# Talking-heads attention and a squared-ReLU FFN: 128-column weights for two matmuls, and another way out for the last output tile

## Chip, cores and metric

The kernel runs on one core of a Trainium2 chip. The metric is the device time of one execution in microseconds. A core has five engines that work side by side, each through its own list of instructions: TensorE (PE, matmuls; its weight loads are shown apart as PEld), VectorE (DVE), ScalarE (ACT), GpSimd (POOL) and SyncE (SP). Transfers run on DMA engines and are issued by GpSimd, SyncE or ScalarE.

## The reference

Eight batches, 12 heads, 448 positions, head size 64. Scores are mixed across the heads before the softmax (w_pre) and again after it (w_post); the result of the attention, 3584 tokens by 768, goes through a feed-forward layer with 2048 inner features.

```python
scores = scale * np.matmul(q, k.transpose(0, 1, 3, 2))
scores = np.einsum('bhij,hg->bgij', scores, w_pre)
scores = scores - np.max(scores, axis=-1, keepdims=True)
attn = np.exp(scores)
attn = attn / (np.sum(attn, axis=-1, keepdims=True) + 1e-09)
attn = np.einsum('bhij,hg->bgij', attn, w_post)
x = np.matmul(attn, v)          # then (b, s, h*d): 3584 x 768
h = np.maximum(x @ w_in, 0.0)   # 768 x 2048
out = h * h @ w_out             # 2048 x 768
```

## The kernel before

A planner in Python puts all work in order before the program is built: each matmul group is a unit, and the planner decides by estimated times which unit TensorE takes next. The built program has a fixed order on every engine.

A batch is handled in chunks of 10 query rows by 12 heads, which is 120 rows (NR). The steps are:

- T: q and k are transposed by TensorE (L610), two heads on top of each other in 128 partitions (`qkt`).
- QK: for a row tile of 12 chunks and a pair of heads, two matmuls, one for the head in partitions 0 to 63 and one for the head in 64 to 127 (L734). The weights are the columns of q, the stream is all 448 columns of k. Both results are copied to `stage`.
- A move by DMA, issued by SyncE (L781), brings a chunk of `stage` into the order "10 rows by 12 heads" on 120 partitions (`dring`).
- Pre-mix: one matmul for each chunk with a block matrix of w_pre as weights (L809), then the exponential with row sums on ScalarE (L827). The first 10 chunks of batch 0 take a direct way (L683).
- Post-mix: four matmuls for each chunk (L873) with w_post scaled by the inverse row sum (L843), then attention times v (L935).
- FFN: the first layer (L994), ReLU, square, second layer (L1076), eviction to `osb`, store.

QK, with the weights i0:i1 of a row tile (the row tiles are 120, 120, 120 and 88 rows; in batch 0 110, 120 and 118, behind the direct chunks):

```python
i0, i1 = ca * CH, min(cb * CH, S)
nr = i1 - i0
...
for par in range(2):
    r0 = par * 64
    r_ = eng.matmul(
        ps[0:nr, banks[par], 0:S],
        qkt[r0:r0 + 64, pb, p, 0, i0:i1],       # weights: 64 rows, nr columns
        qkt[r0:r0 + 64, pb, p, 1, :],           # stream: 448 columns
        start=True, stop=True,
    )
```

Pre-mix:

```python
wk1 = sb("wk1", [NR, CH, H], DT.bfloat16)       # 120 x 120
...
return eng.matmul(ps[0:NR, bank, 0:S], wk1[:, :, :], dring[:, slot, :],
                  start=True, stop=True)
```

The end of an output tile (128 tokens by 768, in two halves of 384 columns): after the second half the whole tile is stored by GpSimd, in as many pieces as the rows of the output need. The last tile, number 3 of the last batch, holds 64 rows of each of two batches and leaves in two pieces:

```python
t_oe = add("oev%d_%d_%d" % (b, tile, hh), FLEX, fn_oe, ...)   # eviction of a half
if hh == 1:
    if b % 2 and tile == 3:
        spans = ((0, b, 384, 448), (64, b - 1, 384, 448))
    ... # cut: pieces of the rows
    def fn_od(eng, en, s=s, pieces=tuple(pieces)):
        for p0, m, row in pieces:
            dst = bass.AP(out.tensor, row * F, [[RJ * F, m], [OP, 4], [1, OP]])
            eng.dma_start(dst, osb[p0:p0 + m, s, :, 0:OP]).then_inc(
                sem_out[s].handle, 16)
    t_od = plan.add("odma%d_%d" % (b, tile), POOL, fn_od,
                    [oev_of[(b, tile, 0)], t_oe], ...)
```

At the very end SyncE waits for the semaphores of all stores.

Of the kernel before, what the change touches and what calls it, by code (L numbers as in the profile page):

```python
# [8 lines left out]
DT = mybir.dt  # L9

PE = "pe"
ACT = "act"
DVE = "dve"
POOL = "pool"
SP = "sp"
FLEX = "flex"
ENGINE_NAMES = (PE, ACT, DVE, POOL, SP)
SEM_LAT = 60.0
MODE_SWITCH = 100.0
ACT_BIAS = 50.0  # L20
MARGIN = 500
MARGIN_DMA = 4000
# [59 lines left out]
class _Plan:  # L82
# [19 lines left out]
    def add(self, name, engine, fn, deps=(), cost=None, prio=0.0, sem=None, seminc=0,  # L102
# [11 lines left out]
        if engine == PE:  # L114
            assert t.nwait == 0
            start = max(self.free[PE], t.avail)
            if t.mode != self.mode:
                start += MODE_SWITCH
                self.mode = t.mode
# [55 lines left out]
    def take(self, n):  # L175
        _, got = self.find(n, self.free[PE])
        self.taken.update(got)
        return got, [t for i in got for t in self.bank_users[i]]
# [11 lines left out]
    def _pick(self):  # L190
# [4 lines left out]
        for s in self.streams:  # L195
# [15 lines left out]
            if u.mode != self.mode:  # L211
                est += MODE_SWITCH
            if est < INF:
# [54 lines left out]
def bass_talking_heads_attention__then__ffn_squared_relu_kernel(  # L268
# [10 lines left out]
    B, H, S, D = q.shape  # L279
    F, FF = moe_w_in.shape  # L280
    assert H == 12 and D == 64 and F == H * D and S == 448 and B % 2 == 0
    CH = 10
    NR = CH * H
# [10 lines left out]
    RJ = 4  # L294
    JB = S // RJ
    NFT = F // 128
    NFFT = FF // 128
    FH = F // 2
# [5 lines left out]
    with ExitStack() as es:  # L304
        def sb(name, shape, dtype):
            return es.enter_context(nc.sbuf_tensor(name, list(shape), dtype))

        def pp(name, shape, dtype):
            return es.enter_context(nc.psum_tensor(name, list(shape), dtype))
# [5 lines left out]
        OP = F // 4  # L315
# [12 lines left out]
        wrep = sb("wrep", [NR, 2, H], DT.float32)  # L328
        wq = sb("wq", [128, NP, H], DT.float32)
        wall = sb("wall", [128, NP, 2, H], DT.float32)  # L330
        wk1 = sb("wk1", [NR, CH, H], DT.bfloat16)
        wk2b = sb("wk2b", [NR, H, CH], DT.bfloat16)
        wk2s = sb("wk2s", [NR, NWS, NR], DT.bfloat16)
        rowsum = sb("rowsum", [NR, NPS, 1], DT.float32)
# [6 lines left out]
        qkt = sb("qkt", [128, 2, NP, 2, S], DT.bfloat16)  # L341
        stage = sb("stage", [IT, 2, H, S], DT.bfloat16)
        dring = sb("dring", [NR, NDS, S], DT.bfloat16)
# [6 lines left out]
        osb = sb("osb", [128, NOS, 4, OP + 8], DT.float32)  # L350

        NB = 8
        ps = pp("ps", [128, NB, 512], DT.float32)
        ps_bf = ps.bitcast(DT.bfloat16)

        def Sm(name):
            return _Sem(nc.alloc_semaphore(name), name)
# [6 lines left out]
        sem_wq = Sm("dwq")  # L364
        sem_w = [[Sm("dw%d_%d" % (i, j)) for j in range(NWP)] for i in range(2)]
        sem_dsl = [Sm("dsl%d" % i) for i in range(NDS)]
        sem_out = [Sm("oslot%d" % i) for i in range(NOS)]

        plan = _Plan(NB)
# [11 lines left out]
        def add(name, engine, fn, deps, cost, prio, mode=None):  # L381
            return plan.add(name, engine, fn, deps, cost, prio, "ctr", 1, mode)
# [5 lines left out]

        def fn_init(eng, en):
            eng.memset(mask[:, :], 1.0)  # L390
            eng.memset(pring[:, :, S:S + 16], 0.0)
            return eng.memset(ident[:, :], 0.0)

# [45 lines left out]
                            sem_w0, 32)  # L439

        def fn_wk1(eng, en):
            o = wk1[:, :, :]
            i0 = wrep[:, 0, :].unsqueeze(1).to_broadcast([NR, CH, H])
            i1 = mask[:, :].unsqueeze(2).to_broadcast([NR, CH, H])
            return eng.scalar_tensor_tensor(o, i0, scale, i1, op0=ALU.mult, op1=ALU.mult)
# [260 lines left out]
        def qtiles(b):  # L706
            return QT if b else QT0
# [6 lines left out]
        def unit_QK(b, T, p):  # L714
            pb = b % 2
            ca, cb = qtiles(b)[T]
            i0, i1 = ca * CH, min(cb * CH, S)
            nr = i1 - i0
            n = n_qt[(b, T)]
            sl = n % 2  # L720

            def needs():
                if (b, p) not in trev or (n >= 2 and rel_left.get(n - 2) != 0):
                    return None
                return [trev[(b, p)]] + stage_reader.get(n - 2, [])

            def go():
                banks, freed = take(2)

                def fn_qk(eng, en):  # L730
                    r_ = None
                    for par in range(2):
                        r0 = par * 64
                        r_ = eng.matmul(  # L734
                            ps[0:nr, banks[par], 0:S],
                            qkt[r0:r0 + 64, pb, p, 0, i0:i1],
                            qkt[r0:r0 + 64, pb, p, 1, :],
                            start=True, stop=True,
                        )
                    return r_  # L740

                t_qk = add("qk%d_%d_%d" % (b, T, p), PE, fn_qk, [trev[(b, p)]] + freed,
                           c_mm(1, S, 8.0), 0, "rows")

                def fn_sev(eng, en):
                    return copy(eng, en, stage[0:nr, sl, 2 * p:2 * p + 2, :],
                                ps[0:nr, banks[0]:banks[0] + 2, 0:S])

                t_sev = add("sev%d_%d_%d" % (b, T, p), FLEX, fn_sev,
                            [t_qk] + stage_reader.get(n - 2, []), c_ev(2 * S),  # L750
                            b * 1000.0 + 20 + 10 * T)
                give(banks, [t_sev])
                sev.setdefault((b, T), []).append(t_sev)
                if p == NP - 1:
                    if cb == NCH:
                        qk_done[b] = t_qk
                    stage_reader[n] = []
                    rel_left[n] = 0
                    for c in range(ca, cb):
                        rel_left[n] += 1  # L760
                        g = b * NCH + c
                        if g < NDS + ND or g - NDS in pre_of:
                            emit_rel(g)
                        else:
                            rel_wait.add(g)

            return _Unit(4.0 if n else 3.45, go, needs, 2, "rows", hold=p % 2 == 0)

        rel_wait = set()
# [26 lines left out]
        def unit_pre(g):  # L796
            b, c = divmod(g, NCH)
            slot = g % NDS

            def needs():  # L800
                if g not in rel or (g >= NPS and g - NPS not in post_of):
                    return None
                return [rel[g], t_wk1]

            def go():
                (bank,), freed = take(1)

                def fn_pre(eng, en):
                    return eng.matmul(ps[0:NR, bank, 0:S], wk1[:, :, :], dring[:, slot, :],  # L809
                                      start=True, stop=True)  # L810

                t_pre = add("pre%d_%d" % (b, c), PE, fn_pre,
                            [rel[g], t_wk1] + freed, c_mm(1, S), 0)
                after_pre(g, t_pre, bank)

            return _Unit(3.0, go, needs, 1, dma=True, paced=True)
# [229 lines left out]
        odmas = []  # L1046
# [49 lines left out]
        def after_F2(b, tile, hh, t_o, bank, s):  # L1096
            def fn_oe(eng, en, hh=hh, bank=bank, s=s):
                return copy(eng, en, osb[:, s, 2 * hh:2 * hh + 2, 0:OP],
                            ps[:, bank, 0:FH].rearrange("p (a b) -> p a b", a=2))

            t_oe = add("oev%d_%d_%d" % (b, tile, hh), FLEX, fn_oe, [t_o, o_free.get(s)],
                       c_ev(FH), b * 1000.0 + 700)
            give([bank], [t_oe])
            oev_of[(b, tile, hh)] = t_oe
            if hh == 1:

                if b % 2 and tile == 3:
                    spans = ((0, b, 384, 448), (64, b - 1, 384, 448))
                else:
                    spans = ((0, b, tile * 128, tile * 128 + 128),)  # L1110
                pieces = []
                for p0, bb, x0, x1 in spans:
                    x = x0
                    while x < x1:
                        r, y = divmod(x, JB)
                        m = min(x1 - x, JB - y)
                        pieces.append((p0 + x - x0, m, bb * S + y * RJ + r))
                        x += m
# [7 lines that stand above are left out]
                n = len(pieces)  # L1126
                t_od = plan.add("odma%d_%d" % (b, tile), POOL, fn_od,
                                [oev_of[(b, tile, 0)], t_oe],
                                {POOL: (580.0 * n, 0.0)}, b * 1000.0 + 710,
                                sem_out[s], 16 * n, dma=("load", n * 200.0 + 1000.0, 45.0))  # L1130
                o_free[s] = t_od
                odmas.append(t_od)
# [34 lines left out]
        per_engine, committed = plan.run()  # L1167

        def fn_final(eng, en):
            for s in sem_out:  # L1170
                eng.wait_ge(s.handle, s.count)

        t_fin = plan.add("final", SP, fn_final, odmas, {SP: (10.0, 10.0)}, 1e9)
# [87 lines left out]
```

## Time and profile before

| | us |
|---|---|
| time, three runs | 606.24, 606.57, 602.82 (median 606.24) |
| span of the profiled execution | 604.3 |
| TensorE busy | 585.0 |
| weight loads busy | 393.4 |
| ScalarE, VectorE, GpSimd busy | 446.5, 352.0, 342.9 |
| weight loads of QK with 120 columns (264 of them) | 14.7, each 127 ns |
| weight loads of pre-mix, 120 columns (350 of them) | 44.2, each 133 ns |
| last eviction ends; span ends | 597.99; 604.3 |

A group line of the profile reads: source line, engine, operation, output tile and input tiles, shape, number of instructions, then busy time of the group in us and the mean of one in ns, then the idle time of the engine before them and who ended it. For a weight load `64*120` is rows by columns of the weights. The records of matmuls overlap each other[...]; the distance from start to start says how fast they follow each other. A line of the timeline gives start in us, length in us, engine, line, operation, tiles, and how many instructions are merged in it. A line of the chain gives start, length and whose work it was.

### The profile page before, as it was taken

The numbers are of one execution on the slowest core, as the hardware profiler recorded it, in microseconds if no ns is written. First come the engines' busy times: TensorE is split into PE (matmuls) and PEld (weight loads), VectorE is DVE, ScalarE is ACT, GpSimd is POOL, SyncE is SP. The second block draws the span as 40 slices with busy tenths as digits, with TensorE's granted clock in tenths as the row PEclk, the third lists the DMA queues.
The fourth block names the chain that finished last, engine by engine and source line by source line (L and its number), as shares of the span: only waits on it lengthen the run. The fifth ranks groups of instructions, "written<-read, shape, count | busy, mean of one in ns | idle before, by whom it ended". The sixth has DMA issues, their size and how long they took to land.

```text
span 604.3 us, 15922 instructions
## 1 busy us (share of the span) xinstructions
PE 585.0 (97%) x6024; PEld 393.4 (65%) x6024; DVE 352.0 (58%) x898; ACT 446.5 (74%) x1160; POOL 342.9 (57%) x686
## 2 busy tenths in 40 slices
PE   7988999999999999999999999999999999999995
PEld 3666867686877665666656665657655666666963
DVE  4787675688576755754768655765657445320410
ACT  2778487888787879798977797889788777862621
POOL 8696559368592758645764556574367543851011
PEclk9999899999999999999999999999999999999998
DMA  9999859576986986458743896447554655201112
GB/s 137 188 225 207 138 99 192 127 138 112 162 135 127 172 154 146 84 87 160 170 87 71 155 183 144 78 82 126 127 105 80 101 108 129 66 2 53 28 31 74
DMA packets 95403, 72.40 MB, mean 120 GB/s; under 512 B 6160, under 2 KB 92896, under 8 KB 95328
## 3 DMA queue, kind: packets, MB, share of 16 engines
q0 software_dynamic: 49632, 33.83, 36.1%
q1 hardware_dynamic: 45696, 37.56, 28.4%
q8 instruction: 49, 0.80, 0.5%
q14 instruction: 26, 0.21, 0.1%
HBM read 45.70 MB, written 11.01 MB: 94 GB/s over the span
## 4 chain that ended last, share of the span: by engine, by line
PE 87%; DMA 4%; DVE 2%; ACT 2%; POOL 1%; issue 1%; SPq 1%; POOLq 0%; DVEq 0%
PE ps L1076 24%; PE ps L994 24%; PE ps L873 12%; PE ps L809 10%; PE ps L734 7%; PE ps L935 6%; PE ps L610 3%; DMA dring<-stage 3%; ACT stage L386 1%; SPq L781 1%; DMA kraw<-in_k_dram 1%; DVE w_out_sb L654 1%; DVE stage L387 1%; DVE a2t L387 0%; POOL wk2s L843 0%
## 5 line engine op out<-in xcount | busy, mean ns | idle before, releaser
L827 ACT ACTIVATE pring<-ps 120x448 bf16<-120x448 f32 x360 | 190.9, 556 | 16.0 <-PE ps L809 13.2
L994 PE MATMUL ps<-xt,w_in_sb 128*128 128x448 bf16 (+6 forms) x1248 | 175.2, 283 | 2.5 <-issue 2.3
L843 POOL TENSOR_SCALAR wk2s<-wk2b,rinv 120x120 bf16<-120x120 bf16 x350 | 124.2, 364 | 85.8 <-DVE rinv L837 82.9
L1076 PE MATMUL ps<-w_out_sb,h2t 128*128 128x384 bf16 x896 | 165.2, 326 | 0.0
L387 DVE CAST a2t<-ps 112x480 bf16<-112x480 f32 x195 | 124.8, 650 | 46.3 <-PE ps L873 44.5
L1032 POOL TENSOR_TENSOR h2t<-h1t 128x448 bf16<-128x448 bf16 (+6 forms) x176 | 114.2, 659 | 48.0 <-ACT h1t L1022 24.1
L994 PEld LDWEIGHTS ps<-xt,w_in_sb 128*128 128x128 bf16 x1248 | 100.9, 99 | 42.3 <-issue 8.0
L873 PE MATMUL ps<-wk2s,pring 120*128 120x120 bf16 x1440 | 119.2, 216 | 1.6 <-POOL wk2s L843 0.5
L873 PEld LDWEIGHTS ps<-wk2s,pring 120*128 120x128 bf16 x1440 | 93.6, 97 | 41.1 <-issue 5.0
L1076 PEld LDWEIGHTS ps<-w_out_sb,h2t 128*128 128x128 bf16 x896 | 83.4, 98 | 55.3 <-issue 6.1
L386 ACT ACTIVATE a2t<-ps 112x480 bf16<-112x480 f32 x165 | 92.5, 575 | 28.9 <-PE ps L873 27.2
L837 DVE RECIPROCAL rinv<-rowsum 120x1 f32<-120x1 f32 x360 | 53.3, 157 | 93.5 <-ACT pring L827 92.7
L386 ACT ACTIVATE stage<-ps 120x896 bf16<-120x896 f32 (+3 forms) x99 | 88.9, 917 | 24.4 <-PE ps L734 23.8
L387 DVE CAST stage<-ps 120x896 bf16<-120x896 f32 (+2 forms) x87 | 93.6, 1086 | 21.4 <-PE ps L734 20.8
L809 PE MATMUL ps<-dring,wk 120*120 120x448 bf16 x350 | 94.3, 356 | 2.1 <-DMA dring<-stage 1.9
L1123 POOL DMA_DIRECT2D out_dram<-osb x56 | 35.3, 633 | 88.6 <-ACT osb L386 76.4
L827 ACT ACTIVATION_READ_ACCUMULATOR pring<-ps 120x1 f32 x360 | 79.6, 221 | 0.0
L1023 DVE TENSOR_SCALAR h1t<-ps 128x448 bf16<-128x448 f32 (+6 forms) x111 | 43.7, 396 | 34.5 <-PE ps L994 29.4
L734 PE MATMUL ps<-qkt 64*120 64x448 bf16 (+3 forms) x372 | 57.7, 376 | 1.3 <-ACT stage L386 0.5
L1022 ACT ACTIVATE h1t<-ps 128x448 bf16<-128x448 f32 (+5 forms) x97 | 42.6, 442 | 20.5 <-PE ps L994 19.8
L809 PEld LDWEIGHTS ps<-dring,wk 120*120 120x120 bf16 x350 | 44.2, 133 | 19.8 <-issue 2.8
L386 ACT ACTIVATE osb<-ps 128x384 f32<-128x384 f32 x35 | 17.2, 490 | 35.6 <-PE ps L1076 35.1
(40 smaller groups left out, 357.2 us busy)
## 6 DMA issues: line engine op xcount, KB each, us to landing
dring<-stage SPq DMA_DIRECT2D x342, 105.0 KB
vraw<-in_v_dram POOLq DMA_DIRECT2D x24, 224.0 KB, 6.2
qraw<-in_q_dram POOLq DMA_DIRECT2D x23, 224.0 KB, 6.5
kraw<-in_k_dram POOLq DMA_DIRECT2D x23, 224.0 KB, 8.3
w_in_sb<-in_moe_w_in_dram POOLq DMA_DIRECT2D x8, 384.0 KB, 9.9
w_out_sb<-in_moe_w_out_dram POOLq DMA_DIRECT2D x12, 256.0 KB, 32.5
out_dram<-osb POOLq DMA_DIRECT2D x8, 336.0 KB, 3.7
out_dram<-osb POOLq DMA_DIRECT2D x8, 288.0 KB, 4.1
```

The lines of the kernel that those rows point to most:

```text
L386: return eng.activation(o, i_, AF.Copy)
L387: return eng.tensor_copy(o, i_)
L734: r_ = eng.matmul(ps[0:nr, banks[par], 0:S], qkt[r0:r0 + 64, pb, p, 0, i0:i1], qkt[r0:r0 + 64, pb, p, 1, :], start=True, stop=True,)
L809: return eng.matmul(ps[0:NR, bank, 0:S], wk1[:, :, :], dring[:, slot, :], start=True, stop=True)
L827: return eng.activation(pring[:, pr, 0:S], ps[0:NR, bank, 0:S], AF.Exp, accum_out=rowsum[:, pr, :])
L837: return eng.reciprocal(rinv[:, pr, :], rowsum[:, pr, :])
L843: return eng.tensor_scalar(wk2s[:, ws, :], wk2b[:, :, :].rearrange("p a b -> p (a b)"), rinv[:, pr, :], 1.0, op0=ALU.mult, op1=ALU.mult)
L873: r_ = eng.matmul(ps[0:128, bank, jb * NR:(jb + 1) * NR], pring[:, pr, jb * JB:jb * JB + 128], wk2s[:, ws, :], start=True, stop=True,)
L994: r_ = eng.matmul(ps[:, bank, 0:n], w_in_sb[:, ft, t16 * 128:(t16 + 1) * 128], xt[:, ft, c0:c1], start=(ft == 0), stop=(ft == NFT - 1),)
L1023: return eng.tensor_scalar(h1t[:, s, 0:n], ps[:, bank, 0:n], 0.0, None, op0=ALU.max)
L1032: return eng.tensor_tensor(h2t[:, t16, o0:o0 + n], h1t[:, s, 0:n], h1t[:, s, 0:n], ALU.mult)
L1076: r_ = eng.matmul(ps[:, bank, 0:FH], h2t[:, t16, col:col + 128], w_out_sb[:, t16, hh * FH:(hh + 1) * FH], start=(t16 == 0), stop=(t16 == N ...
```

## The change

Weights of QK and pre-mix are made 128 columns wide where that is possible. For QK the eight columns behind the row tile are taken along, and their results are not read. For pre-mix the block matrix gets eight zero columns. The last row tile of each batch has no columns behind it and keeps its width. Wider weights are meant to let TensorE load them in its quicker way.

The last output tile is no longer stored as a whole by GpSimd. Each half is stored after its own eviction, in two pieces of 64 rows: three of the four pieces are issued by SyncE, and the second piece of the second half by ScalarE. This is meant to shorten the way from the last matmul to the end.

The diff, cut to its core:

```diff
-MODE_SWITCH = 100.0
+MODE_SWITCH = 100
...
-        wk1 = sb("wk1", [NR, CH, H], DT.bfloat16)
+        wk1 = sb("wk1", [NR, 128], DT.bfloat16)
...
+        sem_last = Sm("olast")
...
             eng.memset(mask[:, :], 1.0)
+            eng.memset(wk1[:, NR:128], 0.0)
...
-            o = wk1[:, :, :]
+            o = wk1[:, 0:NR].rearrange("p (a b) -> p a b", a=CH)
...
+                m = 128 if i0 + 128 <= S else nr
...
-                            ps[0:nr, banks[par], 0:S],
-                            qkt[r0:r0 + 64, pb, p, 0, i0:i1],
+                            ps[0:m, banks[par], 0:S],
+                            qkt[r0:r0 + 64, pb, p, 0, i0:i0 + m],
...
-                    return eng.matmul(ps[0:NR, bank, 0:S], wk1[:, :, :], dring[:, slot, :],
+                    return eng.matmul(ps[0:128, bank, 0:S], wk1[:, :], dring[:, slot, :],
...
-            if hh == 1:
+            if b == B - 1 and tile == 3:
+                for x, (p0, bb) in enumerate(((0, b), (64, b - 1))):
+                    row = bb * S + (384 % JB) * RJ + 384 // JB
+
+                    def fn_ol(eng, en, s=s, p0=p0, row=row):
+                        dst = bass.AP(out.tensor, row * F + hh * FH,
+                                      [[RJ * F, 64], [OP, 2], [1, OP]])
+                        eng.dma_start(dst, osb[p0:p0 + 64, s, 2 * hh:2 * hh + 2, 0:OP]
+                                      ).then_inc(sem_last.handle, 16)
+
+                    en = ACT if hh and x else SP
+                    odmas.append(plan.add("odlast%d_%d" % (hh, x), en, fn_ol, [t_oe], ...))
+            elif hh == 1:
...
-            for s in sem_out:
+            for s in sem_out + [sem_last]:
                 eng.wait_ge(s.handle, s.count)
```

The first two lines change how a number is written and not its value.

## The prediction

> **What bounds the kernel now.** I read the shares of the engines first, then the chain of work that ended last, then the groups of instructions by shape, then the start times of single matmuls, and at the end the last ten microseconds.
>
> ```profile
> PE 585.0 (97%) x6024; PEld 393.4 (65%) x6024; DVE 352.0 (58%) x898; ACT 446.5 (74%) x1160; POOL 342.9 (57%) x686
> ...
> PE 87%; DMA 4%; DVE 2%; ACT 2%; POOL 1%; issue 1%; SPq 1%; POOLq 0%; DVEq 0%
> ```
>
> TensorE is busy for 97% of the span, and 87% of the chain is its matmuls: the order of its instructions is the kernel's length. A busy matmul row is no proof of a full array, though, because the records overlap. So I took the distance from the start of one matmul to the start of the next. In the steady part it is 189 ns for 448 columns, 162 ns for 384 and 52 ns for 120, which is the columns at 2.4 per ns plus about 2 ns. Where the distance is longer, TensorE loses time. From 90 us on, I find only some 4 us of waits for other engines or transfers in it; before 90 us there are about 15 us of them (cold start, loads of weights). What TensorE saves after 90 us should therefore reach the end; what it saves earlier can be swallowed.
>
> What the change touches on TensorE are the weight loads of two lines, L809 (pre-mix) and L734 (QK), in the view of groups that keeps shapes apart:
>
> ```profile
> L873 PEld LDWEIGHTS ps<-wk2s,pring 120*128 120x128 bf16 x1440 | 93.6, 97 | 41.1 <-issue 5.0 <-POOL wk2s L843 4.7 <-ACT pring L827 1.4
> ...
> L809 PEld LDWEIGHTS ps<-dring,wk 120*120 120x120 bf16 x350 | 44.2, 133 | 19.8 <-issue 2.8 <-ACT a2t L386 1.4 <-ACT stage L386 1.0
> ...
> L734 PEld LDWEIGHTS ps<-qkt 64*120 64x120 bf16 x264 | 14.7, 127 | 17.6 <-issue 3.0 <-ACT stage L386 2.7 <-DVE rinv L837 1.8
> ...
> L734 PEld LDWEIGHTS ps<-qkt 64*88 64x88 bf16 x84 | 3.9, 114 | 6.4 <-issue 3.0 <-ACT stage L386 0.6 <-DVE a2t L387 0.5
> ```
>
> The second number after the bar is the mean load in ns. 120 columns take 133, 128 columns take 97: the wider load is 36 ns shorter. Among the QK loads, 32 columns more cost 13 ns. So with 128 columns another, quicker way of loading is in use. The question is how much of a load shows between matmuls.
>
> ```profile
> L734 PE MATMUL ps<-qkt x372: 349/383/398, 9.6 to 503.1; 64*120 64x448 bf16 x132, 64*88 64x448 bf16 x42, 64*110 64x448 bf16 x6, 64*118 64x448 bf16 x6
> ```
>
> ```profile
> 263.23 0.32 PE L873 MATMUL ps<-wk2s,pring 120*128 120x120 bf16 x3
> 263.48 0.59 PE L734 MATMUL ps<-qkt 64*120 64x448 bf16 x4
> 264.00 0.28 PE L873 MATMUL ps<-wk2s,pring 120*128 120x120 bf16 x2
> ```
>
> The first line is shortest, median and longest QK matmul. The second fence is a run of two QK pairs, from 263.48 to 264.00: 520 ns for two streams of 187. By single starts: 145 ns from the last L873 matmul to the first QK matmul instead of 52 (93 lost on entering), 3 ns to its partner in the other half of the rows, 234 ns to the second pair instead of 187 (47 lost), 282 ns to the next L873 (93 lost on leaving). Runs of one pair lose the 47 ns on leaving (329 instead of 282), and in runs of three pairs the third follows after 186. So 47 ns are lost once for each run. With 88 columns it is 34 ns (220 instead of 233 or 234), 13 ns less, as in the loads. It is also the spread of the QK records, 398 against 349. This is the load of the second half of the rows in the first pair, which nothing hides. The 93 ns on entering and leaving are the same for 88 and 120 columns, so they are no load.
>
> **What the Trainium skill says.** "TensorE: Matmul & The Clock Gate", section "Weight-path perf modes — Fast Weight Load (FWL) and DoubleRow", says that the fast load is on by itself when the number of weights is 128 and the type isn't fp32, four times as fast in theory and about two measured. The trace agrees on the direction (97 against 133 ns). "TensorEngine Tiling (Array Packing)", "Gotcha 2: Feature Incompatibilities", excludes fast loads for column tiling; it doesn't list row tiling, which QK uses. No load of 64 rows by 128 columns is in this trace. The first page, "The mechanism", says that a load overlaps running matmuls only for another row group; the trace disagrees: pre-mix matmuls on the same rows follow each other in 189 ns, though each has a load of 133. "DMA: Bandwidth & Descriptors", "Latency and other measured facts", gives about 0.6 us to the first byte from a hardware queue and about 1 us from GpSimd. Here the first packet came 1.0 us after SyncE's first load and 1.2 us after GpSimd's last store, so the gap looks smaller.
>
> **The change part by part.** The order of instructions on TensorE is the same in both programs; only widths differ. **QK**: 276 of 372 matmuls become 128 wide (264 of 120, 12 of 110); the last row tile of each batch (88, and 118 in batch 0) has no columns to spare and stays. The stream of 448 columns is unchanged. A run should lose 47 − 36 = 11 ns instead of 47. After 90 us I count 62 runs that change: 62 × 36 ns = 2.2 us; four of them end in a wait anyway, so 2.1. Before 90 us there are 14: 0.5 us, of which I count half, 0.2. **Pre-mix**: 350 loads become 36 ns shorter, 12.6 us of PEld busy time, but they are hidden. L873 to L809 takes 52 ns as L873 to L873 does, L809 to L809 takes 189 as L994 to L994. Only leaving L809 shows 191 to 192 against 189: at most 161 × 2.5 ns = 0.4 us; I count 0.1. **The new memset** of 8 columns on VectorE lies in the start, before the first loads have landed: 0. TensorE together: 2.4 us.
>
> **The last output tile.**
>
> ```profile
> 597.47 0.02 issue
> 597.49 0.50 ACT osb L386
> 597.99 0.28 issue
> 598.27 0.63 POOL out_dram L1123
> 598.91 0.63 POOLq L1213
> ```
>
> ```profile
> wall<-in_w_pre_dram SPq DMA_DIRECT2D x1, 72.0 KB, 3.0
> ```
>
> The first is the end of the chain, the second an issue by SyncE with its time to landing. The last eviction ends at 597.99, and GpSimd then issues two stores one after the other until 599.54. Their packets end at 601.70, SyncE sees them at 602.08, but GpSimd's closing drain lasts until 604.12 and the span until 604.3: 6.3 us from eviction to end. Now the first half leaves after its own eviction (near 595.4), and the second half's two stores go out together on SyncE and ScalarE, each 64 rows by 1536 bytes = 98 KB. About 0.1 us to the issue; 3.0 us to landing by the row above, or 3.6 as for the last move on that queue (517.9 to 521.5); 0.4 us to close. That is 3.5 to 4.1 us, a gain of 2.2 to 2.8; I take 2.6. GpSimd's last store is then that of the tile before, packets until 596.5, and its drain should be over by about 599 (again 2.4 us later), so it no longer ends the kernel.
>
> Sum: 2.4 + 2.6 = 5.0 us; 606.2 − 5.0 = 601.2, rounded to 601.0.
>
> **The rivals.** (1) The loads are hidden as a whole and TensorE gains nothing: 606.2 − 2.6 = 603.6. The 13 ns between 88 and 120 columns, seen on the array's own starts, speak against it. (2) Entering and leaving also get quicker, as if the 93 ns were load: 76 runs × 186 ns = 14 us, 587. Equal losses at 88 and 120 columns speak against. (3) The fast load doesn't suit pairs in two halves of the rows, and the partners follow each other instead of running together: 138 pairs × 187 ns = 26 us, 632. Nothing in the trace shows this case, and nothing speaks for it. (4) The hardware queues' store takes as long as GpSimd's way: 603.8. (5) TensorE's saving meets waits further on (transfers into the ring, evictions): up to 2 us less gain. (6) The start differs: at 58.7 us TensorE stands 2.3 us, in the page put down to issue, and then runs 3.4 us at half clock. One of the three times before is 3.7 us shorter, about this size (2.3 + 1.7); whether it is this stall, the trace can't say. If the changed kernel mostly misses it, 597.
>
> **Range and chances.** The terms of 2.4 and 2.6 are each good to about 1 us; rival 6 and the spread of 3.7 us of the times before set the width: 597 to 604. Over 2% faster needs 12 us, which only rival 2 gives: 0.04. Over 2% slower needs rival 3 or an unseen stall: 0.02. Within 2%: 0.94.
>
> **What would show each step.** The loads of L734 with 128 columns at about 91 ns and of L809 at 97; PEld busy falls by about 20 us (626 loads by 36 ns are 22, some of them overlapping), the span by 5. Second QK pair about 197 ns after the first instead of 234, single pairs left after 293 instead of 329; entering still 145. L809 to L809 still 189. At the end, from last eviction to end about 3.7 us instead of 6.3, and GpSimd in no part of the chain's end. The prediction is wrong if the 93 ns move, if partners no longer start 3 ns apart, or if another wait of over 1 us appears after 90 us.

## The result and the profile after

The changed kernel took 596.69 us (median of four runs, 596.17 to 597.55) against 604.53 us for four runs of the kernel before (602.55 to 606.57); the ratio is 0.9872, with a 95% interval of 0.9827 to 0.9916. That is 7.8 us less, where 5.0 were predicted, and 0.3 us below the range. Two later series gave 599.22 us (six runs beside 15 of before, ratio 0.9906, 0.9880 to 0.9932) and 599.24 us (six beside 11, ratio 0.9906, 0.9871 to 0.9941). So the change is worth 5.0 to 5.7 us (the difference of these medians, and 0.94% of 604), and the first four runs lay lower than the kernel does on the whole. Most of what follows is about why.

The shares of the engines, and the chain of the changed kernel (a q behind an engine is its sequencer, which waits and issues):

```profile
PE 580.4 (98%) x6024; PEld 377.4 (63%) x6024; DVE 351.5 (59%) x899; ACT 446.4 (75%) x1160; POOL 342.3 (58%) x684
...
PE 88%; ACT 3%; DMA 3%; DVE 2%; POOL 1%; SPq 1%; issue 1%; ACTq 0%; POOLq 0%
```

TensorE still sets the length. Its weight loads are busy for 16 us less (about 20 were predicted), and its span is 9.1 us shorter (604.3 to 595.2); how much of the one is in the other, only the starts of matmuls can tell. The loads that became 128 wide, in the groups by shape (line numbers moved by four; L813 was L809, L738 was L734):

```profile
L813 PEld LDWEIGHTS ps<-dring,wk 120*128 120x128 bf16 x350 | 32.5, 97 | 27.0 <-ACT pring L831 2.9 <-issue 2.5 <-ACT stage L387 1.3
...
L738 PEld LDWEIGHTS ps<-qkt 64*128 64x128 bf16 x276 | 10.8, 93 | 21.0 <-ACT stage L387 2.7 <-issue 2.5 <-DVE rinv L841 2.0
```

133 ns became 97 and 127 became 93. The quick way works for 64 rows, which no row of the trace before could show. And the same run of two QK pairs as was shown in the prediction, in the timeline:

```profile
258.83 0.32 PE L877 MATMUL ps<-wk2s,pring 120*128 120x120 bf16 x3
259.08 0.55 PE L738 MATMUL ps<-qkt 64*128 64x448 bf16 x4
259.57 0.59 PE L877 MATMUL ps<-wk2s,pring 120*128 120x120 bf16 x8
```

From 259.08 to 259.57 it takes 490 ns instead of 520. By single starts the second pair follows after 196 to 197 ns instead of 234, and single pairs are left after 292 instead of 329, as predicted to 1 ns. Entering takes 148 ns instead of 145 and partners still start 3 to 4 ns apart. So the 93 ns for leaving stayed, and entering costs 96 now.

The end of the changed kernel, in the timeline:

```profile
587.87 0.58 POOL L1141 DMA_DIRECT2D out_dram<-osb  x1
...
589.56 3.20 SPq L1116 DMA_DIRECT2D out_dram<-osb  x3
591.64 0.49 ACT L387 ACTIVATE osb<-ps 128x384 f32<-128x384 f32 x1 [2.11 <-PE ps L1080]
592.16 0.74 ACTq L1116 DMA_DIRECT2D out_dram<-osb  x1
```

GpSimd's last store is that of the tile before; its drain ends at 592.96 and nobody waits for it. The last eviction ends at 592.13, the two last stores are issued at 592.16, their last packet ends at 594.39, SyncE sees them at 594.75, and the span ends at 595.2: 3.1 us after the eviction, where it was 6.4.

Where, then, do the remaining microseconds come from? Compare the same matmul in both traces (the order is the same, so the nth matmul is the same work). At 50 us of before the changed kernel is 0.4 us late; at 65 us it is 3.7 us early, of which 0.2 are gone again at 95 us; from there to the last matmul it gains a further 2.3 us, and the end brings 3.3. The 4.1 us between 50 and 65 us are one place in the trace of before, in TensorE's timeline and in a table by stretches (busy time of PE, PEld, DVE, ACT, POOL, then the granted clock, which is 1 at full speed, DMA share, GB/s):

```profile
57.88 1.00 PE L994 MATMUL ps<-xt,w_in_sb 128*128 128x100 bf16 x19
61.19 1.06 PE L994 MATMUL ps<-xt,w_in_sb 128*128 128x100 bf16 x15 [2.31 <-issue]
```

```profile
61.60:65.00 3.40, 3.40 (x46) 3.40 (x43) 1.84 (x7) 0.00 (x0) 2.23 (x7) 0.50 0.79 154
```

Between two matmuls of the same group, with no semaphore to wait for, TensorE stands still from 58.67 to 61.19, and then runs 3.4 us at half clock, which loses about another 1.7. In the changed kernel the same matmuls run through:

```profile
58.28 2.90 PE L998 MATMUL ps<-xt,w_in_sb 128*128 128x100 bf16 x62
```

In the list of transfers, packets of 16 KB come on a queue of its own kind, the "instruction" queue 8, 49 of them (0.80 MB) in each of the two traces:

```profile
q8 instruction: 49, 0.80, 0.5%
```

TensorE has 12,576 recorded instructions, which is 49 packets of 256 (12,544) and a few more. In the trace before the packet that the stalled matmul needs starts at 58.91, after the stall began; in the changed kernel's it starts at 56.32, with 139 instructions still to go. This made the suspicion: TensorE had run out of instructions.

### The profile page after: what moved, and what is told of

It is laid out like the page before. It is cut to its first block, busy times and chain, and to the rows that moved or that the text cites. A ratio compares the mean times of both kernels' runs of the same rounds, so it can differ in the third digit from the quotient of the medians.

```text
span 595.2 us, 15926 instructions
## 1 busy us (share of the span) xinstructions
PE 580.4 (98%) x6024; PEld 377.4 (63%) x6024; DVE 351.5 (59%) x899; ACT 446.4 (75%) x1160; POOL 342.3 (58%) x684
## 4 chain that ended last, share of the span: by engine, by line
PE 88%; ACT 3%; DMA 3%; DVE 2%; POOL 1%; SPq 1%; issue 1%; ACTq 0%; POOLq 0%
PE ps L1080 24%; PE ps L998 24%; PE ps L877 12%; PE ps L813 11%; PE ps L939 7%; PE ps L738 7%; PE ps L612 3%; ACT stage L387 2%; DMA dring<-stage 2%; DMA kraw<-in_k_dram 1%; SPq L785 1%; ACT pring L831 1%; DVE w_out_sb L656 1%; DVE stage L388 1%; DVE a2t L388 0%
## 5 line engine op out<-in xcount | busy, mean ns | idle before, releaser
L998 PE MATMUL ps<-xt,w_in_sb 128*128 128x448 bf16 (+6 forms) x1248 | 173.4, 281 | 0.2 <-DVE h1t L1027 0.2
L998 PEld LDWEIGHTS ps<-xt,w_in_sb 128*128 128x128 bf16 x1248 | 98.9, 97 | 41.1 <-issue 5.7
L813 PE MATMUL ps<-dring,wk 120*128 120x448 bf16 x350 | 93.8, 353 | 2.8 <-ACT pring L831 1.6
L1141 POOL DMA_DIRECT2D out_dram<-osb x54 | 34.1, 634 | 84.1 <-ACT osb L387 72.1
L738 PE MATMUL ps<-qkt 64*128 64x448 bf16 (+2 forms) x372 | 54.7, 359 | 1.5 <-ACT stage L387 0.5
L813 PEld LDWEIGHTS ps<-dring,wk 120*128 120x128 bf16 x350 | 32.5, 97 | 27.0 <-ACT pring L831 2.9
```

Source lines behind the costliest of these rows:

```text
L738: r_ = eng.matmul(ps[0:m, banks[par], 0:S], qkt[r0:r0 + 64, pb, p, 0, i0:i0 + m], qkt[r0:r0 + 64, pb, p, 1, :], start=True, stop=True,)
L813: return eng.matmul(ps[0:128, bank, 0:S], wk1[:, :], dring[:, slot, :], start=True, stop=True)
L998: r_ = eng.matmul(ps[:, bank, 0:n], w_in_sb[:, ft, t16 * 128:(t16 + 1) * 128], xt[:, ft, c0:c1], start=(ft == 0), stop=(ft == NFT - 1),)
```

## The experiments

The times of before in the first series are 44 runs with a median of 604.30 us (602.4 to 607.6); in the later ones the medians are 604.37, 604.19 and 604.22. These four series ran on four different chips, so the chip makes no difference to the kernel before that could be seen; on which chip the first four runs of the changed kernel were taken is not on record. Where a diff "takes back" something, the lines are those of the change.

### Weights alone

```diff
 # the kernel before, with the weights of QK and pre-mix as changed
-t_oe per half: stores by SP, SP, SP, ACT      (taken back)
+after the second half: two stores by POOL     (as before)
```

> The 128-column weights of QK and pre-mix alone, the last tile stored as before. Theory A (the wider weights are worth 2.3 us of TensorE after 90 us and nothing more; the 4 us stall of TensorE near 58 us is an instruction fetch that comes late by chance, in any kernel of this layout): runs without the stall near 602.7 - 2.4 = 600.3 us, runs with it near 604.3, and the clock of a run tells which (0.994 with, 0.999 without). Theory B (the wider weights themselves take the stall away): no run with the stall, all near 600.3. Theory C (the wider weights are worth more than the steady part shows): under 599.5 without the stall.

Measured: 602.34 us (22 runs, 600.46 to 605.70), ratio 0.9968 (0.9954 to 0.9981), so 1.9 us less, with 1.1 to 2.8 in the interval. The 2.4 us predicted lie inside. The profiled run had the stall at the same instruction, 0.6 us long, so theory B of the expectation is out: the wider weights don't remove it. The clock of a run did not tell the stall as I had written: runs at 0.993 were among the shortest and one at 0.998 had 603.1. The profiled run had half clock at 10.3 us and after the last matmul, neither near the stall.

### The way out of the last tile alone

```diff
 # the kernel before, with the new stores of the last tile
-ps[0:m, ...], qkt[..., i0:i0 + m], wk1[:, :] 120x128   (taken back)
+ps[0:nr, ...], qkt[..., i0:i1], wk1[:, :, :] 120x120   (as before)
```

> The new way out of the last tile alone. Theory A: from the end of the last eviction to the end of the span 3.0 us instead of 6.3, so 602.7 - 3.3 = 599.4 us without the stall and 603.4 with it; TensorE untouched. If the stall is tied to the wider weights (theory B), about half of these runs have it, as before. If my recorded 2.6 us for this part were right: 600.1.

Measured: 600.13 us (6 runs, 599.53 to 603.69), ratio 0.9931 (0.9905 to 0.9957). The profile has 3.1 us from last eviction to end, so 3.3 us are gained there, inside the interval of 2.6 to 5.7. This end hardly varies: it is 3.06 to 3.09 us in all eight profiles of kernels with the new stores and 6.36 to 6.48 us in all four with the old ones. The profiled run is the longest of the six, and its timeline has three stalls of the suspected kind; the last line below follows the second of them:

```profile
66.68 1.06 PE L936 MATMUL ps<-a2t,vraw 112*64 112x110 bf16 x36
68.37 0.48 PE L936 MATMUL ps<-a2t,vraw 112*64 112x110 bf16 x12 [0.63 <-issue]
```

They stand at TensorE's recorded instructions 1217, 1473 and 1729, that is 256 apart, in three different lines (first FFN layer, attention times v, transposes).

### QK alone, pre-mix alone

```diff
 # QK alone: the kernel before with
+m = 128 if i0 + 128 <= S else nr      # and m for nr in the matmul
 # pre-mix alone: the kernel before with
+wk1 = sb("wk1", [NR, 128], DT.bfloat16)      # eight zero columns
```

> Only QK takes 128-column weights. Theory A: 2.2 us less than before without the stall (62 runs of pairs after 90 us by 36 ns), so 600.5; second pair of a run after 197 ns instead of 234. Rival: the gain comes from pre-mix, then under 1 us here.

> Only pre-mix takes 128-column weights. Theory A: its loads fall from 133 to 97 ns each and the time stays within 0.5 us of before without the stall (602.2 to 602.8), since the loads were hidden. Rival: 350 loads by 36 ns = 12.6 us, or a good part of it, show up in the time.

QK alone: 601.96 us (7 runs), ratio 0.9955 (0.9934 to 0.9976), 2.7 us less with 1.4 to 4.0 in the interval; its second pairs follow after the 197 ns, and a run of two pairs takes 490 ns:

```profile
258.88 0.55 PE L736 MATMUL ps<-qkt 64*128 64x448 bf16 x4
259.37 0.44 PE L875 MATMUL ps<-wk2s,pring 120*128 120x120 bf16 x5
```

Pre-mix alone: 603.91 us (22 runs), ratio 0.9998 (0.9985 to 1.0011), though its loads fell as they should:

```profile
L810 PEld LDWEIGHTS ps<-dring,wk 120*128 120x128 bf16 x350 | 32.5, 97 | 26.7 <-issue 2.8 <-ACT pring L828 1.4 <-ACT a2t L386 1.3
```

So 350 loads shorter by 36 ns, 12.6 us in sum, bring nothing that can be told from the times, whose interval reaches from 0.9 us less to 0.7 us more. The traces resolve more, matmul by matmul against before from 95 us on: QK alone gains 1.9 us, through the one load for each run of pairs that isn't hidden; pre-mix alone gains 0.7 us, of which 0.4 lie where TensorE leaves a pre-mix matmul for another kind (133 places, 3 ns each) and the rest in waits between pre-mix matmuls. The 0.4 us stand in the trace of the changed kernel too. QK brings most of the gain of the weights, then, and not all of it.

### The changed kernel again

No edit.

> The changed kernel once more, beside more runs of before. The first experiments showed before spread from 602.4 to 607.6 (median 604.3), with a stall of TensorE near 59 us that is 0.6 to 2.5 us long where it is there. Theory A (the parts add up: 2.0 from the weights, 3.3 from the tail, the rest was luck in the four runs that had 596.2 to 597.6): a median near 599, lowest runs near 596.3, and some runs 2 to 4 us above those. Theory B (with all parts together the stall is gone): all runs within 596 to 598, median near 596.8.

Measured: 599.22 us (6 runs, 597.76 to 600.94), ratio 0.9906 (0.9880 to 0.9932). Theory A holds for the median, near 599, and for the spread of 3.2 us; its lowest runs near 596.3 did not come (the lowest is 597.8). The profiled run has no stall of the packet kind, but two stretches at half clock that the first profile of the changed kernel lacks (from 10.9 and from 147.4 us, 3.4 us each), the second after a distance of 2.2 us between two pre-mix matmuls at 144.6 us, where the second waits for a move into the ring; it is 1.6 us in the first profile and 1.5 us in that of before.

### What of the new way out brings the gain

```diff
 # whole tile, SyncE and ScalarE
-stores after each half: SP, SP; SP, ACT (64 rows x 384 columns each)
+stores after the second half: SP; ACT (64 rows x 768 columns each)
 # halves, GpSimd
-en = ACT if hh and x else SP
+en = POOL
```

> The changed kernel, but the last tile leaves as a whole after its second half: 64 rows each through SyncE and ScalarE, 196 KB each. Theory (what counts is that GpSimd's two issues and its closing drain leave the end): from the end of the last eviction to the end of the span 3.5 to 4.0 us, against 3.0 with halves and 6.3 before; so about 0.7 us slower than the changed kernel. Rival (what counts is that half of the tile leaves early): 5 us or more.

> The changed kernel, the last tile in halves, but all four pieces issued by GpSimd. Theory (GpSimd's issues of 0.63 us one after the other and its drain of 2.4 us behind the last packet set the end): 5.3 to 6.0 us from the end of the last eviction to the end of the span. Rival (the early half counts): 3.5 to 4 us.

Whole tile through SyncE and ScalarE: 4.1 us from last eviction to end (594.64 to 598.7), just over the 3.5 to 4.0 expected and far from the rival's 5. Halves through GpSimd: 6.0 us (594.06 to 600.0). Against 6.4 before and 3.1 with both, halves alone bring 0.4 us, the other queues alone 2.3, both 3.3. The end of the chain with GpSimd and halves looks as it did before:

```profile
593.57 0.50 ACT osb L387
594.07 0.29 issue
594.36 0.60 POOL out_dram L1116
594.96 0.59 POOLq L1231
```

GpSimd's drain then ends at 599.8, and the span 0.2 us later. The two medians, 598.69 us (4 runs) and 600.98 (8 runs), ratios 0.9901 (0.9872 to 0.9930) and 0.9945 (0.9925 to 0.9965), agree with this for GpSimd. The whole-tile kernel's median is 0.5 us below that of the changed kernel beside it, though its end is 1.0 us longer; with four and six runs that vary by 2 to 3 us, the medians can't decide this, and the ends in the profiles do.

### Moving the packets

```diff
 # the changed kernel; the first warm-up group
-for _ in range(n):                       # 16 matmuls of 448 columns
+w = 4 if n == 16 else 1
+for _ in range(n * w):                   # 64 matmuls of 112 columns
```

> The changed kernel with 96 more TensorE instructions in the first warm-up group (64 matmuls of 112 columns instead of 16 of 448), so that every later 16 KB packet of TensorE instructions begins 96 instructions earlier in the work. Theory A (the stall near 59 us is TensorE running out of instructions): no stall between matmul 585 and 586 of the old count any more; if there is one, it stands 96 instructions earlier in the work, or where a later packet begins. Rival (it waits for weights or for another engine at that matmul): if there is a stall near 59 us, it stands at the same matmul of the first FFN layer with 100 columns as in before. Time within 2 us of the changed kernel either way.

Measured: 599.80 us (4 runs, 599.14 to 600.90), ratio 0.9910 (0.9878 to 0.9943). The FFN matmuls with 100 columns run through. Now the long stall is in the matmuls with 110 columns:

```profile
67.80 0.71 PE L999 MATMUL ps<-xt,w_in_sb 128*128 128x110 bf16 x11
70.39 0.22 PE L999 MATMUL ps<-xt,w_in_sb 128*128 128x110 bf16 x1 [1.88 <-issue]
```

It is TensorE's recorded instruction 1729 of this program too, while the work at that place is 96 instructions earlier than it was in the experiment with the last tile alone, where 1729 was a transpose. The stall belongs to the packet and not to the matmul, its weights or another engine.

The transfers confirm it in all fourteen profiles. Instruction 1217 is the first one of the fourth packet on the queue, and every 256 further on begins the next. In the eleven stalls (three in the run with the last tile alone, two in the one with halves through GpSimd, one in each of six others) the first instruction starts 1.32 to 1.62 us after its packet's transfer has ended; without a stall it is never sooner than 1.33 us, and mostly much later. A packet begins to move when some 240 instructions are still to go (the medians of the fourteen profiles are 232 to 245). In the FFN matmuls with 100 columns, 240 instructions last about 5.3 us by 44 ns for two, an estimate; a packet that comes a few us late then stops TensorE.

### Fewer bytes beside the packets

```diff
 # the changed kernel; loads of w_out
-[[F, 128], [128 * F, nt], [1, WC]]     # 256 columns for each piece
+[[F, 128], [128 * F, nt], [1, 64]]     # 64 of them
+memset of the part of w_out_sb that nothing else writes, on VectorE at the start
```

> The changed kernel, but of every four columns blocks of w_out only the first quarter is loaded (256 bytes of each 1024), the rest is filled with zeros or left as it was, so the second layer's weights are incomplete; the order of instructions is the same. It takes 4.7 MB of transfers out of the stretch from 40 to 80 us. Theory (packets of TensorE instructions come late there because they queue behind the loads of weights): no stall over 0.3 us at a packet's first instruction, the packet before the FFN matmuls with 100 columns is fetched with over 150 instructions left, and the median is 1.5 to 3 us below the changed kernel (599.2), near 597 or lower, with a spread under 2 us. Rival (the fetch is late for a reason of its own): the stalls and the spread stay, median near 599.

Measured: 597.46 us (6 runs, 596.66 to 601.94), ratio 0.9900 (0.9871 to 0.9929). The profiled run has no stall at a packet, and the packet in question starts with 173 instructions left, as expected; but two of the six runs are long, 600.0 and 601.9, against the expected spread under 2 us, and the ratio can't be told from the changed kernel's. That the loads of weights make the packets late is therefore not shown.

### Two attempts at a better kernel

```diff
 # row tiles of QK, all with 128 columns
-QT = ((0, 12), (12, 24), (24, 36), (36, NCH))
+QT = ((0, 12), (12, 24), (24, 32), (32, NCH))
+QT0 = ((ND, 21), (21, 32), (32, NCH))
 # first FFN layer of batch 0 in two groups
-groups = [(p,) for p in parts_of(b)] if b in split else [parts_of(b)]
+groups = ([parts_of(b)[0:2], parts_of(b)[2:4]] if b == 0 else
+          [(p,) for p in parts_of(b)] if b in split else [parts_of(b)])
```

> The changed kernel with other row tiles of QK, so that the last one of a batch also has 128 columns (320 to 447) and the third takes 128 with room behind it. Theory (a run of pairs loses what its second weight load shows, 34 ns at 88 columns, 11 at 128): 23 runs by 23 ns = 0.5 us, so a ratio to before near 0.990, not to be told from the changed kernel (0.9906) unless the planner's other order costs or gains more.

> The changed kernel with the first FFN layer of batch 0 in two groups of 230 and 218 columns instead of four of 130, 100, 110 and 108: 384 TensorE instructions fewer between 40 and 90 us, and 98 ns for each matmul where it was 44. Theory (TensorE runs out of instructions in these short matmuls): no stall at a packet's first instruction near 60 us, median 1 to 3 us below the changed kernel. Rival (waiting for the larger group costs what the stall cost): no gain or a loss of some us.

Measured: 600.99 us (6 runs), ratio 0.9942 (0.9925 to 0.9960), and 601.84 us (8 runs), ratio 0.9958 (0.9936 to 0.9980). Neither profiled run has a stall at a packet, and in the second there are only 47 packets. Both medians lie above the changed kernel's 599.2 all the same. The order of TensorE's matmuls is another one in both, and new waits came, in the second for the pre-mix matmuls (1.1 to 1.3 us from start to start at 211, 226 and 279 us); that these waits are the whole difference was not shown. Neither beats the changed kernel.

### The changed kernel a third time

No edit.

> The changed kernel a third time, beside more runs of before, to settle whether its true distance from before is the 7.8 us of the first four runs or the 5.2 us of the next six. Theory A (sum of the parts, 2.0 + 3.3 us, the first four runs were lucky in their stalls): ratio 0.990 to 0.9925, median 598 to 600. Theory B (the parts together also remove stalls): ratio 0.986 to 0.9885, median near 597.

Measured: 599.24 us (6 runs, 597.56 to 602.02), ratio 0.9906 (0.9871 to 0.9941). Theory A again. Its profiled run has the stall of the kernel before, at the same instruction 1217 and of the same length, and the half clock after it:

```profile
58.82 0.82 PE L998 MATMUL ps<-xt,w_in_sb 128*128 128x100 bf16 x15
61.96 0.73 PE L998 MATMUL ps<-xt,w_in_sb 128*128 128x100 bf16 x13 [2.32 <-issue]
```

```profile
63.30:66.70 3.40, 3.40 (x45) 3.40 (x42) 1.98 (x8) 0.00 (x0) 2.81 (x9) 0.50 0.79 156
```

Its span is 599.3 us, 4.1 more than that of the first profile of the same program, which had neither. Matmul by matmul it is 0.4 us behind that profile before the stall (it also has half clock from 8.7 us on) and 4.0 behind at 70 us: the stall and the half clock make nearly all of it.

## Why the prediction was right and wrong

**What bounds the kernel**: right. TensorE's order is the length, and what QK saved after 90 us reached the end.

**QK, 2.1 us after 90 us and 0.2 before**: right. The single distances came out as worked out (197 and 292 ns), the trace gives 2.3 us from 95 us on for both kinds of weights, 1.9 us for QK alone, and QK alone measured 2.7 with 1.4 to 4.0 in the interval. The inference that carried it was that the part of a run which depends on the columns (34 ns at 88, 47 at 120) is load, and the part that doesn't (93 ns) is not. Rivals 1, 2 and 3 are out by the starts, rival 4 by the end of 3.1 us.

**Pre-mix, 0.1 us**: right that the loads are hidden, with the small part mis-sized. The 0.4 us that the prediction gave as the most for leaving L809 are there in the traces; the times (0.9998) can't tell 0.1 from 0.4.

**The last tile, 2.6 us**: right mechanism, mis-sized term. It measured 3.3. The mis-sized piece is the time to landing, taken as 3.0 to 3.6 us from a load at the start and a move in a loaded stretch. Here it was 2.6 us from issue (592.16) to SyncE's release (594.75), with two quarters of the tile on two queues and nothing else on the way.

**The sum, "606.2 − 5.0 = 601.2"**: this is the step that failed, and the failing term is the 606.2, not the 5.0. The base was the median of three runs, two of them near 606.4, and the profiled execution (606.1) had the stall near 59 us and the half clock behind it; the sum carries them over, as if they belonged to both kernels. Four series of 11 to 44 further runs put the kernel before at 604.2 to 604.4, and 604.3 − 5.0 = 599.3 is where twelve later runs of the changed kernel lie (599.2). The first four, at 596.7, lay 2.5 us below that, and their one profile has neither stall nor half clock before its last matmul. The 9.1 us between the two first profiles are therefore 2.3 for the weights, 3.3 for the end and 4.1 for the stall and the half clock, less 0.6 that the changed kernel lost elsewhere up to 95 us. Rival 6 named the stall, its place and its size (2.3 + 1.7 us), but I let it only widen the range, whose lower end of 597 has no room for a term that is too small: 601.2 − 4.0 and the 0.7 us that the last tile brought more would be 596.5.

The experiments show what the stall is. In the six profiles that have one near 59 us it is at TensorE's instruction 1217, and all distances between matmuls from 50 to 100 us that are over 0.33 us too long with no semaphore behind them are at 1217, 1473 or 1729 (one of 0.5 us after a packet's stall lies in a stretch of half clock); 96 added instructions move them in the work, and each ends 1.3 to 1.6 us after the packet has come. The stall comes and goes in one and the same program, so it is no effect of the change. Why a packet comes late in one execution and not in the next stays open; the one experiment on it was inconclusive. That the first four runs of the changed kernel lay so low is then luck, as far as the record shows. They had no half clock to speak of (0.999 to 1.0 for each), and the one profile among them no stall; whether all four had none, only the times suggest.

**Rival 5**, waits further on: seen at one place. The distance that is 1.5 us in the profile of before (149.1 us) is 1.6, 2.2 and 1.8 us in the three profiles of the changed kernel, so 0.2 to 0.8 us are lost there. It is no steady loss of the wider weights: the two kernels that send the last tile out in another way have them too and stand there for 1.4 us.

## What to carry to other kernels

Read what a weight load costs from the distance between starts of matmuls, not from its busy time: here 12.6 us of shorter loads brought 0.7 us at most, and 36 ns once for each run of QK pairs brought 1.9 us. The last store is worth its own look: here it paid to take it off an engine that issued its stores one after the other and whose drain ended the program (2.3 of 3.3 us). And before adding a saving to a base of three runs, ask what in the profile comes and goes by itself: here a stall of one engine with no semaphore behind it was worth 4.1 us with the half clock after it, against 5.0 to 5.7 for the whole change.

## What was not expected of the hardware

- TensorE can run out of instructions. Its program comes in packets of 16 KB, 256 instructions each; in a stretch of short matmuls (two instructions in each 44 ns) with busy DMA queues, a late packet stopped it for 0.5 to 2.8 us, until 1.3 to 1.6 us after the packet had come.
- After three of the five stops of over 2 us, and after a wait of 2.2 us, the granted clock was 0.5 for 3.41 us, which lost up to 1.7 us more. After the other two (2.5 and 2.8 us) it stayed at 1; what decides is open.
- Already in the trace of before: going from matmuls on all rows to pairs in two halves of the rows costs 93 to 96 ns, going back 93, for weights of 88, 120 and 128 columns; with the 102 runs of QK pairs in this kernel that is about 19 us.
- GpSimd's closing drain ended 2.3 to 2.4 us after the last packet of its last store in thirteen profiles (601.70 to 604.12 in that of before), and 2.9 us after it where GpSimd stored the last tile in four pieces.
